# Strassen's weight sums made in place over two blocks, and one activation sum split into the double-buffered operand

## The chip, the cores and the metric

The kernel runs on one core of one Trainium2 chip. The metric is the device time of one execution in microseconds (us); the time of a kernel is the median of its runs. The core has a matrix engine (TensorE, PE in the profile), a vector engine (VectorE, DVE), a scalar engine (ScalarE, ACT), GpSimd (POOL) and a queue of DMA issues (SyncE, SP). Each engine takes its own instructions strictly in order; engines wait for each other by semaphores.

## The reference

Inputs and outputs are fp32 with 8 samples of 576 tokens and 512 channels. Three stages follow each other: a compressed attention, a mixer with two two-layer nets, and a mixture of four causal attention experts. The change lies in the second net of the mixer:

```python
u = x + h.transpose(0, 2, 1)
h2 = np.maximum(u @ w_ch1, 0.0) @ w_ch2      # w_ch1: 512 x 1536, w_ch2: 1536 x 512, given as 64-bit floats
return (u + h2).astype(np.float32)
```

## The kernel before

Every fp32 operand is split into a high part in the rounded type fp32r and the remainder (`split`: ScalarE rounds, VectorE subtracts); a product is then three matmuls, high x high, high x low and low x high (`mm3`). The 1536 hidden channels are 12 chunks of 128 (`fc`). Chunks 0 and 1 are done in the first stage, chunks 10 and 11 in the last one, chunks 2 to 9 in the stage of the change, which walks over 9 blocks of 512 tokens (`n`). The weights come as 64-bit floats, one load per chunk and matrix, into two staging buffers (`cst`), and are converted by a chain of steps on ScalarE and VectorE (`f64_split`, lines 120 to 129): line 120 on ScalarE and 124 on VectorE read a load that has landed, line 127 is the last to read it and so frees its staging buffer for the load after the next.

In blocks 0, 7 and 8 a chunk's hidden layer is a plain product (`mm1`); its eviction is `hh` on ScalarE (line 638) and `hl` on VectorE (line 639). In blocks 1 to 6 (`WIDE`) two chunks and two halves of the tokens are a 2 x 2 product of blocks, done in seven products instead of eight by the Strassen-Winograd scheme (`mm1w`). It needs, once for all blocks, four sums of weights for each of the four pairs of chunks `q` (`sums_w`: GpSimd joins the parts of both weights at line 655, makes four half-size sums at lines 659 to 663, and `split` makes `sh` and `sl` of them), and for each block four sums of activations (`split_q`: in place in `ub` on GpSimd, lines 679 to 685), each split once more: `split_t` makes `th` and `tl` of all four at the end of the block before, two of the `tl` on VectorE and two on GpSimd. `th` and `tl` have one buffer, so they wait until the last product of the block before has read them; the operand `uh`, `ul` of the plain quadrants has two. The products are added up on VectorE (lines 712 to 726) and evicted as `hh` and `hl` (lines 646 and 647). The second layer (`mm2`, four banks `o`) follows one step behind and is added to the partial result `pb` at the end of a block (line 742).

All weight sums are emitted in block 0, two steps per chunk. Their temporaries, two `x` and one `s` of four quarters, are a pool of their own (`stmp`), freed at the end of block 0; the temporaries `m1` to `m5` of the products (`uw`) then take its place. At the build a scheduler sets the order of each engine's instructions: it may place one far ahead of where it was emitted, as soon as its operands and its memory are free. So it has placed the first pairs' sums into the first stage, and the first steps of four loads for chunks 10 and 11 into block 0, although these chunks come hundreds of microseconds later.

## Time and profile before

| | |
|---|---|
| Time, median of 3 runs | 1232.45 us (1229.34 to 1232.87) |
| Profiled execution | 1230.86 us, of which the span from first to last instruction is 1229.2 |
| Busy share of the span | TensorE 97%, VectorE 66%, ScalarE 51%, GpSimd 37% |
| Block 0 on the trace | from 344 to 398 us, then block 1 |
| Granted TensorE clock, mean | 0.994 of full speed |

A matmul's end is modelled, so a row's duration is longer than the distance to the next one; what counts is where TensorE stands idle, and the distance of the starts. Engines other than TensorE may idle at no cost as long as nothing is late for it.

### The profile page before, as it was taken

Reading aid. Unit: us, or ns where it says so; the run is one execution under the profiler, and the core shown is the slowest. Engines: PE = TensorE matmul, PEld = TensorE weight load, DVE = VectorE, ACT = ScalarE, POOL = GpSimd, SP = SyncE. Lnnn points to the kernel's source line nnn. Section 1 sums busy time; section 2 is a strip of 40 time slices with the busy share of each in tenths; the row PEclk is TensorE's granted clock in tenths of the full one; section 3 lists DMA queues with packets and bytes.
Section 4 is the critical chain, followed back from the end, with each engine's and each line's share of the span. In section 5 each row is a group of like instructions: output and inputs, shape, how many; then the busy total and the mean of one; then the engine's idle time right before and its main releaser. Section 6 shows DMA issues by size and latency. Waiting matters only on the chain.

```text
span 1229.2 us, 24045 instructions
## 1 busy us (share of the span) xinstructions
PE 1186.2 (97%) x8730; PEld 1105.1 (90%) x8730; DVE 812.6 (66%) x1989; ACT 624.6 (51%) x1651; POOL 459.4 (37%) x646
## 2 busy tenths in 40 slices
PE   5789999999999999999999999999999999999998
PEld 4789999999987889888998888999999999999987
DVE  6877787886588676666555214676766766677774
ACT  3554656656344232222222113677676767676775
POOL 1432525446017122122105304454544546373421
PEclk9899999999999999999999999999999999999999
DMA  9875857753263231232134403332333233322423
GB/s 247 219 195 167 233 168 188 210 148 106 100 234 129 70 103 36 69 104 77 61 103 112 149 15 111 73 97 78 82 87 83 78 82 86 117 72 76 119 59 112
DMA packets 159765, 143.00 MB, mean 116 GB/s; under 512 B 73120, under 2 KB 128672, under 8 KB 159648
## 3 DMA queue, kind: packets, MB, share of 16 engines
q1 hardware_dynamic: 159648, 141.47, 39.8%
q8 instruction: 69, 1.13, 0.4%
q14 instruction: 48, 0.39, 0.1%
HBM read 90.05 MB, written 39.85 MB: 106 GB/s over the span
## 4 chain that ended last, share of the span: by engine, by line
PE 79%; DVE 5%; DMA 5%; POOL 3%; ACT 3%; issue 3%; SPq 1%; DVEq 0%; ACTq 0%; POOLq 0%
PE g L98 29%; PE o L98 13%; PE h L98 12%; PE b L98 8%; PE y L1134 4%; PE s L1025 2%; PE t L1089 2%; PE s L373 2%; DMA cst<-in_moe_w_ch_dram 2%; PE g L300 1%; PE s L1047 1%; DMA ub<-u_d 1%; DMA cst<-in_moe_w_tok_dram 1%; PE t L356 1%; PE g L468 1%
## 5 line engine op out<-in xcount | busy, mean ns | idle before, releaser
L98 PE MATMUL o<-hl,w2h 128*128 128x512 f32 x288 | 114.0, 396 | 2.5 <-DVE hl L639 2.3
L98 PE MATMUL o<-hh,w2l 128*128 128x512 f32 x288 | 113.1, 393 | 0.0
L1070 POOL TENSOR_TENSOR a<-a,cf 128x128 f32<-128x128 f32 (+3 forms) x128 | 88.1, 723 | 64.6 <-DVE cf L1062 56.5
L98 PE MATMUL o<-hh,w2h 128*128 128x512 f32 x288 | 108.3, 395 | 0.9 <-ACT hh L638 0.6
L646 ACT ACTIVATE hh<-m 128x256 fp32r<-128x256 f32 x96 | 38.7, 415 | 112.0 <-DVE m L717 74.3
L1014 DVE CUSTOM_DVE_ANT_0 ssb<-s,cmask 128x128 f32<-128x128 f32 (+2 forms) x144 | 68.4, 482 | 28.2 <-PE s L1025 14.1
L1027 ACT ACTIVATE a<-ssb,nb 128x128 f32<-128x128 f32 (+3 forms) x128 | 71.4, 558 | 19.1 <-DVE nb L1014 16.4
L389 POOL TENSOR_TENSOR at<-ssb,ssm 128x640 f32<-128x640 f32 x16 | 21.5, 1344 | 158.6 <-DVE ks L316 77.2
L923 POOL TENSOR_TENSOR xl<-p,xh 128x288 fp32r<-128x288 f32 x60 | 47.7, 811 | 84.1 <-ACT xh L922 84.0
L98 PE MATMUL g<-xh,qkh 128*128 128x288 f32 x256 | 76.1, 302 | 0.0
L98 PE MATMUL g<-xl,qkh 128*128 128x288 f32 x256 | 75.8, 297 | 0.0
L98 PE MATMUL g<-xh,qkl 128*128 128x288 f32 x256 | 75.1, 295 | 0.0
L647 DVE SCALAR_TENSOR_TENSOR hl<-m,hh 128x256 fp32r<-128x256 f32 x96 | 58.1, 615 | 17.3 <-ACT hh L646 15.6
L694 POOL TENSOR_TENSOR tl<-ub,th 128x512 fp32r<-128x512 f32 x12 | 18.5, 1562 | 133.2 <-ACT th L693 133.2
L98 PE MATMUL h<-ul,w1h 128*128 128x512 f32 (+2 forms) x200 | 66.8, 334 | 0.0
L98 PE MATMUL h<-uh,w1l 128*128 128x512 f32 (+2 forms) x200 | 66.8, 334 | 0.0
L98 PEld LDWEIGHTS o<-hl,w2h 128*128 128x128 f32 x288 | 54.6, 189 | 13.6 <-DVE hl L639 3.1
L98 PE MATMUL h<-uh,w1h 128*128 128x512 f32 (+2 forms) x200 | 66.6, 334 | 0.0
L98 PEld LDWEIGHTS o<-hh,w2h 128*128 128x128 f32 x288 | 54.0, 189 | 12.2 <-DVE pb L742 1.2
L98 PEld LDWEIGHTS o<-hh,w2l 128*128 128x128 f32 x288 | 54.5, 189 | 11.3
L105 DVE TENSOR_TENSOR Bl<-t,Bh 128x512 fp32r<-128x512 f32 (+1 forms) x80 | 50.4, 634 | 18.3 <-ACT Bh L102 17.4
L639 DVE SCALAR_TENSOR_TENSOR hl<-h,hh 128x512 fp32r<-128x512 f32 x24 | 16.5, 687 | 63.5 <-ACT hh L638 63.5
(325 smaller groups left out, 4382.7 us busy)
## 6 DMA issues: line engine op xcount, KB each, us to landing
cst<-in_moe_w_ch_dram SPq DMA_DIRECT2D x24, 512.0 KB, 4.9
u_d<-u SPq DMA_DIRECT2D x32, 288.0 KB, 2.2
p_d<-u SPq DMA_DIRECT2D x16, 576.0 KB, 3.5
ub<-u_d SPq DMA_DIRECT2D x9, 1024.0 KB, 5.3
pb<-p_d SPq DMA_DIRECT2D x36, 256.0 KB, 3.6
x_d<-pb SPq DMA_DIRECT2D x36, 256.0 KB, 2.2
u<-u_d SPq DMA_DIRECT2D x16, 576.0 KB, 4.2
p<-x_d SPq DMA_DIRECT2D x15, 576.0 KB, 4.0
```

The source lines that it names most:

```text
L98: PE.matmul(ps, lhsT=a, rhs=b, start=start and i == 0, stop=stop and i == len(seq) - 1)
L105: DVE.tensor_sub(lo, src, f(hi))
L373: PE.matmul(p[:, j, 2 * pr:2 * pr + 2, :], lhsT=qT[:, pr, 128 * j:128 * j + 128], rhs=km[:, 64 * pr:64 * pr + 64], start=True, stop=True)
L646: ACT.activation(hh, c, AF.Relu)
L647: DVE.scalar_tensor_tensor(hl, c, 0.0, f(hh), op0=OP.max, op1=OP.subtract)
L923: POOL.tensor_sub(xl[b][:, c, ss], x_, f(xh[b][:, c, ss]))
L1014: DVE.tensor_tensor_reduce(out=out, in0=p, in1=mask, scale=-scale, scalar=least, op0=OP.add, op1=OP.min, accum_out=acc)
L1025: PE.matmul(p[:, 0:W], lhsT=q_[n][:, 128 * c:128 * c + 128], rhs=kk[n][:, 0:W], start=(i == 0), stop=(i == 1))
L1027: ACT.activation(a[:, aoff[c]:aoff[c] + W], s_[:, 0:W], AF.Exp, scale=-1.0, bias=nb[:, 0:1], accum_out=sm[:, c:c + 1])
L1070: POOL.tensor_mul(x_, x_, cf[:, c:c + 1].to_broadcast([128, W]))
L1089: PE.transpose(p[:, 128 * kc:128 * kc + 128], a[:, o + 128 * kc:o + 128 * kc + 128], ident[:])
L1134: PE.matmul(p[:, lo:w], lhsT=v_[:, kc, 0, :], rhs=x, start=(i == 0), stop=(i == len(ops) - 1))
```

## The change

Three things change. The sums of weights use no `s` any more: each is made in place in the two `x`, which become four quarters that `split` reads in another order (`W` picks them by a table). The pairs are emitted in two blocks: pairs 0 and 1 in block 0 (one step per chunk from the third on), pairs 2 and 3 in block 1 (`SOON = 2`), and the pool of temporaries stays open with the operands. Weight conversion steps are emitted two per chunk instead of one. And of the four sums of activations, the one that is the second product's operand (quadrant 2,2 of `ub` after its sum) is split in `split_q` into the fourth quadrant of `uh`, `ul`, which was unused; `th` and `tl` shrink from four quarters to three, of which VectorE makes two `tl` and GpSimd one.

```diff
--- before.py
+++ after.py
@@ -655,16 +655,16 @@
                 POOL.tensor_add(t[:], f(w1h[fc][:]), f(w1l[fc][:]))
             yield
             a11, a12, a21, a22 = x[0][:, 0:2, :], x[0][:, 2:4, :], x[1][:, 0:2, :], x[1][:, 2:4, :]
-            s_ = stmp.tile([128, 4, 2, 128], F32, name="s")
-            POOL.tensor_add(s_[:, 0], a21, a22)
-            POOL.tensor_sub(s_[:, 1], s_[:, 0], a11)
+            POOL.tensor_add(a22, a21, a22)
+            POOL.tensor_sub(a21, a11, a21)
             yield
-            POOL.tensor_sub(s_[:, 2], a11, a21)
-            POOL.tensor_sub(s_[:, 3], a12, s_[:, 1])
+            POOL.tensor_sub(a11, a22, a11)
+            POOL.tensor_sub(a12, a12, a11)
             sh[q] = sw.tile([128, 4, 2, 128], F32R, name=f"sh{q}")
             sl[q] = sw.tile([128, 4, 2, 128], F32R, name=f"sl{q}")
             for i in range(2):
-                split(sh[q][:, 2 * i:2 * i + 2], sl[q][:, 2 * i:2 * i + 2], s_[:, 2 * i:2 * i + 2])
+                split(sh[q][:, 2 * i:2 * i + 2], sl[q][:, 2 * i:2 * i + 2],
+                      x[i][:].rearrange("p (s c) f -> p s c f", s=2))
             yield
 
         def quad(x, j, k):
@@ -683,21 +683,22 @@
             POOL.tensor_sub(q22, q22, q11)
             yield
             POOL.tensor_sub(q21, q21, q22)
+            split(quad(uh[n], 0, 1), quad(ul[n], 0, 1), q22)
             yield
 
         def split_t(n):
-            th[n] = sw.tile([128, 4, 2, 256], F32R, name="th")
-            tl[n] = sw.tile([128, 4, 2, 256], F32R, name="tl")
-            q11, q12, q21, q22 = [quad(ub[n], j, k) for j in range(2) for k in range(2)]
-            for i, q_ in ((1, q22), (2, q12), (0, q11), (3, q21)):
+            th[n] = sw.tile([128, 3, 2, 256], F32R, name="th")
+            tl[n] = sw.tile([128, 3, 2, 256], F32R, name="tl")
+            q11, q12, q21 = [quad(ub[n], j, k) for j, k in ((0, 0), (0, 1), (1, 0))]
+            for i, q_ in ((1, q12), (0, q11), (2, q21)):
                 ACT.activation(th[n][:, i], q_, AF.Copy)
-                (DVE if i in (1, 2) else POOL).tensor_sub(tl[n][:, i], q_, f(th[n][:, i]))
+                (POOL if i == 2 else DVE).tensor_sub(tl[n][:, i], q_, f(th[n][:, i]))
 
         def mm1w(n, q):
             f0, f1 = N1 + 2 * q, N1 + 2 * q + 1
             A = lambda fc, j: [x[fc][:, 2 * j:2 * j + 2, :] for x in (w1h, w1l)]
             U = lambda j, k: [quad(x[n], j, k) for x in (uh, ul)]
-            W = lambda i: [x[q][:, i] for x in (sh, sl)]
+            W = lambda i: [x[q][:, (3, 0, 2, 1)[i]] for x in (sh, sl)]
             X = lambda i: [x[n][:, i] for x in (th, tl)]
 
             def prod(pool, a, b):
@@ -708,9 +709,9 @@
             m1, u2_, u3, u4, c = [uw.tile([128, 256], F32, name=x, bufs=2)[:] for x in ("m1", "m2", "m3", "m4", "m5")]
             p = prod(pp, A(f0, 0), U(0, 0))
             ACT.activation(m1, p, AF.Copy)
-            p = prod(pp, W(1), X(1))
+            p = prod(pp, W(1), U(0, 1))
             DVE.tensor_add(u2_, m1, p)
-            p = prod(ppw, W(2), X(2))
+            p = prod(ppw, W(2), X(1))
             DVE.tensor_add(u3, u2_, p)
             p = prod(ppw, W(0), X(0))
             DVE.tensor_add(u4, u2_, p)
@@ -718,7 +719,7 @@
             p = prod(pp, A(f0, 1), U(1, 0))
             hidden(n, f1, 1, c)
             DVE.tensor_add(m1, m1, p)
-            p = prod(pp, A(f1, 1), X(3))
+            p = prod(pp, A(f1, 1), X(2))
             hidden(n, f0, 0, m1)
             DVE.tensor_add(u3, u3, p)
             p = prod(ppw, W(3), U(1, 1))
@@ -788,16 +789,17 @@
             split_u(0, kd)
         load_u(1)
         b1_ctx.close()
-        sw_ctx, tmp_ctx = ExitStack(), ExitStack()
+        sw_ctx = ExitStack()
         sw = sw_ctx.enter_context(tc.tile_pool(name="sw", bufs=1, side="right", reuse_waits="tile"))
         ppw = sw_ctx.enter_context(tc.tile_pool(name="ppw", bufs=1, space=PSUM, side="right", reuse_waits="tile"))
-        stmp = tmp_ctx.enter_context(tc.tile_pool(name="stmp", bufs=1, side="right", reuse_waits="tile"))
+        stmp = sw_ctx.enter_context(tc.tile_pool(name="stmp", bufs=1, side="right", reuse_waits="tile"))
         NQP = (KM - N1) // 2
         WIDE = range(1, NBLK - 2)
+        SOON = 2
         work = [(n, q) for n in range(NBLK) for q in range(NQP)]
         LAG = 1
         NW = len(work)
-        pending, sprep = [], (x for q in range(NQP) for x in sums_w(q))
+        pending, sprep = [], iter(())
         uw = None
         for i in range(NW + LAG):
             items = [()] if i == NW else [work[i]] if work[i][0] in WIDE else [(*work[i], 0), (*work[i], 1)]
@@ -809,6 +811,8 @@
                         banks(n)
                         prep = iter(()) if n + 1 == NBLK else split_q(n + 1) if n + 1 in WIDE else \
                             (split_u(n + 1, kd) for kd in range(KD))
+                        if n < 2:
+                            sprep = (x for k in range(*((0, SOON), (SOON, NQP))[n]) for x in sums_w(k))
                     if len(it) == 2:
                         mm1w(n, q)
                     else:
@@ -820,8 +824,9 @@
                             load_p(n, fc - KM + KD)
                         if n == 0:
                             next(wcl, None)
-                            for _ in range(2):
-                                next(sprep, None)
+                            next(wcl, None)
+                        if n == 1 or n == 0 and fc > N1 + 1:
+                            next(sprep, None)
                         if n > WIDE[-1]:
                             for _ in range(4):
                                 if next(wcl, 0) == 0 and c2 is None:
@@ -836,8 +841,10 @@
                             for g in (wcl, sprep):
                                 for _ in g:
                                     pass
-                            tmp_ctx.close()
                             uw = sw_ctx.enter_context(tc.tile_pool(name="uw", bufs=1, side="right", reuse_waits="tile"))
+                        if n == 1:
+                            for _ in sprep:
+                                pass
                         if n + 1 in WIDE:
                             split_t(n + 1)
                         if n + 2 < NBLK:
```

How the scheduler's order moves is shown for three places. The first is ScalarE in the second half of block 0. In the rows `hh<-h` are the evictions of hidden chunks 7, 8 and 9, `sh` the copies of weight sums, and `cm<-cst` is line 120 on the hoisted loads, each of which has its own semaphore (DMAHW4, 5, 6 in the order of issue). Before:

```order
L638 ACTIVATE hh<-h 128x512 [waits PE_49,Activation_49]
L120 ACTIVATE cm<-cst 128x512 [waits DMAHW4_49]
L102 ACTIVATE sh_5273<-s 128x512 [waits Pool_49]
L120 ACTIVATE cm<-cst 128x512 [waits DMAHW5_49,DVE_49]
L102 ACTIVATE sh_5273<-s 128x512 [waits Pool_49]
L638 ACTIVATE hh<-h 128x512 [waits PE_49,Activation_49]
L120 ACTIVATE cm<-cst 128x512 [waits DMAHW6_49,DVE_49]
L102 ACTIVATE sh_5320<-s 128x512 [waits Pool_49] x2
L638 ACTIVATE hh<-h 128x512 [waits PE_49,Activation_49]
```

The same place on ScalarE now:

```order
L120 ACTIVATE cm<-cst 128x512 [waits DMAHW4_49]
L638 ACTIVATE hh<-h 128x512 [waits PE_49,Activation_49]
L102 ACTIVATE sh_5352<-x_5281 128x512 [waits DMAHW3_49,DMAHW0_49,Pool_49]
L120 ACTIVATE cm<-cst 128x512 [waits DMAHW5_49,DVE_49]
L102 ACTIVATE sh_5352<-x_5280 128x512 [waits Pool_49]
L120 ACTIVATE cm<-cst 128x512 [waits DMAHW6_49,DVE_49]
L638 ACTIVATE hh<-h 128x512 [waits PE_49,Activation_49]
L102 ACTIVATE sh_5570<-x_5465 128x512 [waits Pool_49]
L102 ACTIVATE sh_5570<-x_5464 128x512 [waits Pool_49]
L638 ACTIVATE hh<-h 128x512 [waits PE_49,Activation_49]
```

The evictions of chunks 7 and 8 each stand behind one more of the loads' steps, and the copies of the fourth pair (5320 before) have gone further down.

The second is GpSimd, from the last of the in-place sums for block 1 on (`ub<-ub`); `x` and `s` are the temporaries, their numbers those of the pairs. Before, with the first pair and half of the second already done in the first stage:

```order
L685 TENSOR_TENSOR ub<-ub 128x2x256 [waits DVE_49,Pool_49]
L659 TENSOR_TENSOR s<-x_5148 128x256 [waits DVE_49]
L662 TENSOR_TENSOR s<-x_5147,x_5148 128x256
L694 TENSOR_TENSOR tl<-ub,th 128x512 [waits PE_49,Activation_49]
L694 TENSOR_TENSOR tl<-ub,th 128x512 [waits Activation_49]
L660 TENSOR_TENSOR s<-s,x_5147 128x256 [waits Pool_49]
L655 TENSOR_TENSOR x_5232<-w1h_4834,w1l_4835 128x512 [waits Pool_49]
L663 TENSOR_TENSOR s<-x_5147,s 128x256 [waits Pool_49]
L655 TENSOR_TENSOR x_5231<-w1h_3318,w1l_3319 128x512 [waits Pool_49]
```

The same place on GpSimd now:

```order
L685 TENSOR_TENSOR ub<-ub 128x2x256 [waits DVE_49,Pool_49]
L655 TENSOR_TENSOR x_5170<-w1h_854,w1l_855 128x512 [waits DMAHW5_49,DMAHW6_49,DMAHW3_49,DMAHW7_49,DMAHW2_49,DMAHW0_49]
L655 TENSOR_TENSOR x_5171<-w1h_882,w1l_883 128x512
L695 TENSOR_TENSOR tl<-ub,th 128x512 [waits PE_49,Activation_49]
L658 TENSOR_TENSOR x_5171<-x_5171 128x256 [waits Pool_49]
L659 TENSOR_TENSOR x_5171<-x_5170,x_5171 128x256 [waits Pool_49]
L661 TENSOR_TENSOR x_5170<-x_5171,x_5170 128x256 [waits Pool_49]
L662 TENSOR_TENSOR x_5170<-x_5170 128x256 [waits Pool_49]
L655 TENSOR_TENSOR x_5281<-w1h_2084,w1l_2085 128x512 [waits DVE_49]
L658 TENSOR_TENSOR x_5281<-x_5281 128x256 [waits Pool_49]
L655 TENSOR_TENSOR x_5280<-w1h_2029,w1l_2030 128x512 [waits DVE_49]
```

All four pairs stand behind the sums for block 1 now, each full-size sum waits for VectorE to have read the same buffer for the pair before, and one `tl` is gone.

The third is VectorE at the start of block 1, from the first sum of the products on; `m` are the sums, `pb` the additions at the end of block 0, `ul<-ub` a split of the sums of activations for block 2. Before:

```order
L712 TENSOR_TENSOR m_5424<-m_5423,h 128x256 [waits PE_49,Activation_49]
L742 TENSOR_TENSOR pb<-o_5086,pb 128x512 [waits PE_49]
L714 TENSOR_TENSOR m_5425<-m_5424,h 128x256 [waits DVE_49]
L716 TENSOR_TENSOR m_5426<-m_5424,h 128x256
L742 TENSOR_TENSOR pb<-o_5087,pb 128x512 [waits PE_49]
L742 TENSOR_TENSOR pb<-o_5088,pb 128x512 [waits PE_49]
L717 TENSOR_TENSOR m_5427<-m_5425,h 128x256 [waits DVE_49]
L742 TENSOR_TENSOR pb<-o_5089,pb 128x512 [waits PE_49]
L720 TENSOR_TENSOR m_5423<-m_5423,h 128x256 [waits PE_49]
L723 TENSOR_TENSOR m_5425<-m_5425,h 128x256 [waits DVE_49,PE_49]
L647 SCALAR_TENSOR_TENSOR hl<-m_5427,hh 128x256 [waits Activation_49]
L726 TENSOR_TENSOR m_5426<-m_5426,h 128x256 [waits PE_49]
```

The start of block 1 on VectorE now:

```order
L105 TENSOR_TENSOR sl_5692<-x_5579,sh_5691 128x512 [waits Activation_49]
L713 TENSOR_TENSOR m_5391<-m_5390,h 128x256 [waits PE_49,Activation_49]
L105 TENSOR_TENSOR sl_5692<-x_5578,sh_5691 128x512 [waits Activation_49]
L715 TENSOR_TENSOR m_5392<-m_5391,h 128x256 [waits DVE_49]
L717 TENSOR_TENSOR m_5393<-m_5391,h 128x256 [waits PE_49]
L743 TENSOR_TENSOR pb<-o_5086,pb 128x512 [waits PE_49]
L718 TENSOR_TENSOR m_5394<-m_5392,h 128x256 [waits DVE_49]
L743 TENSOR_TENSOR pb<-o_5087,pb 128x512 [waits PE_49]
L721 TENSOR_TENSOR m_5390<-m_5390,h 128x256 [waits PE_49]
L743 TENSOR_TENSOR pb<-o_5088,pb 128x512 [waits PE_49]
L105 TENSOR_TENSOR ul<-ub,uh 128x2x256 [waits Activation_49]
L647 SCALAR_TENSOR_TENSOR hl<-m_5394,hh 128x256 [waits Activation_49]
```

The two `sl` of the fourth pair and the new split stand among the first pair's sums and ahead of its first `hl`.

## Rows read from the trace of the kernel before

**Rows 1.** Three stretches: busy us (and instructions) of each engine, granted clock, DMA.
```profile
380.00:390.00 10.00, 8.11 (x32) 6.04 (x31) 9.30 (x10) 2.94 (x5) 8.69 (x8) 0.90 0.62 210
390.00:400.00 10.00, 9.61 (x45) 7.68 (x43) 7.49 (x9) 5.42 (x10) 6.97 (x8) 0.93 0.16 53
...
450.00:460.00 10.00, 10.00 (x61) 8.64 (x60) 7.32 (x17) 1.58 (x4) 1.23 (x1) 1.00 0.63 210
```

**Rows 2.** Waits of TensorE, 310 to 660 us: us in total, times, longest.
```profile
PE o L98 <- DVE hl L639: 2.3, 2, 1.9
PE h L98 <- DVE m L717: 0.9, 1, 0.9
...
PE o L98 <- ACT hh L638: 0.6, 1, 0.6
PE o L98 <- DVE pb L742: 0.3, 1, 0.3
```

**Rows 3.** Timeline of TensorE: start, us, instruction [idle before <-releaser].
```profile
388.08 0.80 PE L98 MATMUL o<-hl,w2h 128*128 128x512 f32 x1 [1.90 <-DVE hl L639]
...
391.23 0.45 PE L98 MATMUL o<-hh,w2h 128*128 128x512 f32 x1
...
391.97 0.40 PE L98 MATMUL h<-uh,w1h 128*128 128x512 f32 x1
...
394.49 0.39 PE L98 MATMUL h<-uh,w1l 128*128 128x512 f32 x1
```

**Rows 4.** Timeline of VectorE, block 0.
```profile
359.64 1.51 DVE L121 TENSOR_SCALAR cm<-cm 128x512 f32<-128x512 f32 x1
...
363.11 0.41 DVE L121 TENSOR_SCALAR cm<-cm 128x512 f32<-128x512 f32 x1
...
377.58 1.52 DVE L124 TENSOR_SCALAR cy<-cst 128x512 int32<-128x512 uint32 x1
...
379.61 1.18 DVE L127 SCALAR_TENSOR_TENSOR cy<-cst,cm 128x512 int32<-128x512 int32 x1
...
387.01 0.41 DVE L124 TENSOR_SCALAR cy<-cst 128x512 int32<-128x512 uint32 x1
...
387.35 0.68 DVE L639 SCALAR_TENSOR_TENSOR hl<-h,hh 128x512 fp32r<-128x512 f32 x1
```

**Rows 5.** Timeline of the DMA queue: issues of two weight loads.
```profile
380.87 0.34 SPq L152 DMA_DIRECT2D cst<-in_moe_w_ch_dram  x1
...
393.09 0.34 SPq L152 DMA_DIRECT2D cst<-in_moe_w_ch_dram  x1
```

**Rows 6.** Timeline of ScalarE, block 0.
```profile
372.99 0.57 ACT L638 ACTIVATE hh<-h 128x512 fp32r<-128x512 f32 x1
...
386.84 0.67 ACT L120 ACTIVATE cm<-cst 128x512 f32<-128x512 f32 x1 [1.45 <-DMA cst<-in_moe_w_ch_dram]
...
393.05 0.58 ACT L638 ACTIVATE hh<-h 128x512 fp32r<-128x512 f32 x1
...
396.70 0.67 ACT L120 ACTIVATE cm<-cst 128x512 f32<-128x512 f32 x1 [3.07 <-DMA cst<-in_moe_w_ch_dram]
```

**Rows 7.** Timeline of GpSimd, end of the first stage and block 0.
```profile
274.49 2.52 POOL L655 TENSOR_TENSOR x<-w1h,w1l 128x512 f32<-128x512 f32 x2 [6.58 <-DVE w2l L129]
...
286.75 1.28 POOL L655 TENSOR_TENSOR x<-w1h,w1l 128x512 f32<-128x512 f32 x1
...
359.25 1.62 POOL L683 TENSOR_TENSOR ub<-ub 128x512 f32<-128x512 f32 x1
...
360.95 1.35 POOL L685 TENSOR_TENSOR ub<-ub 128x512 f32<-128x512 f32 x1
...
373.11 2.05 POOL L659 TENSOR_TENSOR s<-x 128x256 f32<-128x256 f32 x1 [10.80 <-DVE sl L105]
...
377.26 2.99 POOL L694 TENSOR_TENSOR tl<-ub,th 128x512 fp32r<-128x512 f32 x2
...
397.34 0.75 POOL L663 TENSOR_TENSOR s<-x,s 128x256 f32<-128x256 f32 x1
```

## What is predicted

> **What bounds the kernel now.** I read the page's first table, then a table by stretches, then the waits of TensorE, then each engine in order of time where TensorE waited. In the first TensorE fills nearly the whole span, so only time in which it waits or runs slow can be won, or lost by a new wait. The stretches show where that is in the stage that the change touches: from 380 to 400 us TensorE is busy 8.11 and 9.61 of 10 us at a granted clock of 0.90 and 0.93, while VectorE is busy 9.30 and 7.49; at 450, between two wide blocks, it is busy all the time [rows 1]. So the loss sits in block 0 and at the start of block 1 (from 400 us), not in the wide blocks that follow.
>
> The list of TensorE's waits from 310 to 660 us names it: 2.3 us for `hl` of line 639 in two waits, 0.6 for `hh` of line 638, 0.9 for a sum of line 717, and 0.3 at a later block border [rows 2]. The 1.9 us wait costs twice: the seven steps from the matmul of 388.08 to that of 391.23 are 0.45 us each, the eleven from 391.97 to 394.49 0.23 us; the first run at about half the pace, which is the lower of TensorE's two levels (1.2 GHz), right behind the wait, and that adds 7 x 0.22 = 1.6 us [rows 3]. Together 0.6 + 2.3 + 1.6 + 0.9 = 5.4 us: more than that block 0 and its border cannot give back.
>
> Why is `hl` late? VectorE takes its instructions in order. `hl` of 387.35 stands behind a conversion step of line 124 that waits for a weight load [rows 4]; the load was issued at 380.87 [rows 5], and ScalarE, which waits for the same load, goes on at 386.84, 6.0 us later; the next such pair is 393.09 and 396.70, 3.6 us [rows 5, 6]. Four such loads are for the last two hidden chunks, which nobody needs in this stage. The second thing in VectorE's way is GpSimd: line 121 takes 0.41 us alone at 363.11, but 1.51 us at 359.64, ending 0.28 us after the GpSimd instruction that ran from 359.25 to 360.87 [rows 4, 7]. Conversely GpSimd's half-size sum takes 0.75 us at 397.34 and 2.05 us at 373.11, where VectorE works without a gap [rows 7].
>
> **The change part by part.**
>
> *Sums in place.* The number of GpSimd sums is the same: 8 full-size (two take 2.52 us, so 1.26 each) and 16 half-size ones (0.75) [rows 7]. But they move in time. Before, four full-size and four half-size ones run between 274.49 and 288 us, in the first stage (the first and the last of these rows stand in [rows 7]). In the changed order all stand behind the four in-place sums of activations, the last of which begins at 360.95 [rows 7]. So 4 x 1.26 + 4 x 0.75 = 8 us of GpSimd work comes into block 0. GpSimd was idle from 362.3 to 373.11 [rows 7], which hides the first two full-size sums (2.5 us); they now meet VectorE's conversions there, where line 121 ran in 0.41 us. By row 359.64 a VectorE step then loses up to 1.1 us, by row 373.11 none, GpSimd waits instead: bounds 0 and 2.5 us on the conversion chain, and I take 1.
>
> The Trainium skill (SBUF — State Buffer, section "Who interferes with whom") says that whichever of the two engines issues first holds the shared port for its whole instruction, for a VectorE step with two SBUF inputs too. By that every one of the moved sums can push the chain; the chain would slip by the upper bound here, and the trace shows both outcomes (1.51 us at 359.64, and GpSimd's own 2.05 us at 373.11).
>
> *Place a, hidden chunk 5.* Two `sh` and one `th` copy go from ahead of `hh` of 372.99 [rows 6], so the 0.6 us wait for it goes. But the seven matmuls of block 1 that TensorE had put between `hh` and `hl` (they need the first `sh`) now come later, and `hl` is hardly earlier (two `sl` fewer, one split more). TensorE asks for it about 0.9 us after 372.3, it comes at about 374.4: a wait of 1.2 us instead of 0.6. Change +0.6 (bounds -0.6 and +1.5).
>
> *Place b, chunk 6.* `hh` now stands behind the first `sh`, that is behind GpSimd. +0.4 (0 to 2).
>
> *Place c, chunk 7.* Today 1.9 + 1.6 us. In the new order `hl` stands behind three steps of the load of 380.87 instead of one, 0.41 + 0.68 us more, and `hh` behind ScalarE's step on that load. But the load starts earlier: its buffer is released by the line 127 of 379.61, which took 1.18 us, and the line 124 of 377.58 ahead of it 1.52, both behind the two `tl` sums of 377.26 on GpSimd [rows 4, 7]; only one of those is left, and it comes sooner. Without it the two take 0.41 and 0.68, and the load goes 1.6 us earlier, at 379.2. With 4.8 us of flight (the middle of 3.6 and 6.0) and 2.4 us of steps, `hl` is ready at 386.4; TensorE asks at 385.1, counted from 372.3 with 49 matmuls of 0.23 us and the waits of a and b. A wait of 1.3 (0 to 2.6) and some slow clock: 2.0 instead of 3.5. Change -1.5 (-3.5 to 0).
>
> *Place d, chunk 8.* This is the step on which my sign rests. Before, `hh` of 393.05 stands ahead of ScalarE's step on the last load, which goes at 396.70 [rows 6]. In the changed order it stands behind it, and `hl` behind VectorE's step on it. That load's buffer is released only by the line 127 that comes right after `hl` of place c. So from `hl` of c to `hh` of d it takes 0.6 + 3.6 to 6.0 + 0.7 + 0.6 = 5.5 to 7.9 us, more with GpSimd in the way, where TensorE has 23 matmuls of 0.23 us, 5.3 us. A wait of 0.2 to 3.8 us; I take 2.0, with 0.8 of slow clock, instead of 0.4 + 0.1 now. Change +2.3.
>
> *Start of block 1.* The sums of the fourth pair now begin after `sl` of the third, right behind `hl` of d, and mix with the in-place sums for block 2. VectorE and ScalarE in turn have a copy of the fourth pair ahead of the first sums of the products, and a split of `ub` (it waits for the third in-place sum of block 2) ahead of the first `hl`. Counting from `hl` of d with 1.26 and 0.75 us, the fourth pair's second half is ready after 7.5 us and that split after 11.4; TensorE asks for the buffers that hang on them after 9.1, 10.5 and 12.6 us and gets them after about 9.3, 11.8 and 13.0: 1.9 us in three waits, and 5.5 with the mutual slowing of the rows of 359.64 and 373.11. Today 0.9 [rows 2]. I take 3.7; change +2.8 (+1.0 to +4.6).
>
> *Split into the double-buffered operand.* In each of blocks 2 to 6 GpSimd has one `tl` less (1.5 us, the half of 377.26 [rows 7]) and VectorE one split more, which now is made one block earlier instead of at the border. No wait for `tl` is among TensorE's in the wide blocks [rows 2], so nothing is won there. But the extra split falls where the border's sums and additions are, VectorE busy 7.32 of 10 us [rows 1], and the wait listed there is 0.3 us. +0.1 a border on five borders, +0.5 (from -1.5, all of it gone, to +3.5, the whole 0.7 us of the split each time).
>
> Sum: 0.6 + 0.4 - 1.5 + 2.3 + 2.8 + 0.5 = +5.1 us. The profiled execution took 1230.86 us (span 1229.2 and 1.66 around it), so 1236.0 by its measure; the median of the runs, 1232.45, lies 1.6 higher: 1237.5.
>
> **The rivals.** A measurement of this kernel can tell about 0.3%, 3.7 us.
>
> *Traded even.* a to c go as above, but block 1 starts without the mutual slowing (1.9 instead of 3.7), d is served by a 3.6 us flight (0.5 instead of 2.8) and the borders stay: 0.6 + 0.4 - 1.5 + 0.1 + 1.0 + 0.5 = +1.1, so 1233.5. For it speaks that only the short bounds are shown as such by rows; against it that VectorE is busy over 9 of 10 us around 385.
>
> *Faster.* GpSimd starts its sums at 362.3 instead of 373.1, all pairs are ready early, the queue ahead of `hl` shrinks and the long wait with its slow clock never happens. Then a and c give back 0.6 + 3.5, the start of block 1 0.9, and the five borders 0.2 each: -6, so 1226.5. It holds from the point where no wait in block 0 passes 1 us. For it: the idle 10.8 us are real. Against it: every later pair waits for the `sl` of the pair before, so an early start doesn't carry through, and the loads order the chunks anyway.
>
> *Slower by the port.* Each moved sum pushes the conversion chain, as at 359.64, and never the other way round: b +1.4, c -0.3, d +3.8, block 1 +4.6, borders +1.0, with a +11, so 1243.5. It decides from the point where the chain slips by more than 2 us before c. The rule of the Trainium skill named above points this way.
>
> **How the numbers follow.** Forecast (a wait that moves one load nearer and a late fourth pair, +3.7 to +8): 0.40; traded even: 0.35; faster: 0.15; slower by the port: 0.10. Faster by over 0.3%: 0.15; within: 0.37 (the even case and a little of the forecast's lower end); slower: 0.48. The forecast's own range is 1235 to 1241. The range for 8 in 10 leaves out half of the faster case and half of the port case: 1228 to 1244.
>
> **What would show it.** In the changed profile GpSimd's line 655 should begin near 362, not 274; the wait for `hh` at 373 should be gone and one for `hl` stand there; a wait of 1 to 3 us for `hh` or `hl` of line 638 and 639 should end right after ScalarE's step on the last load (place d), and waits for sums of the products should total 2 to 5 us between 400 and 420. If `hh` of d is served before TensorE asks, or the stretch from 400 to 420 is busy throughout, I am wrong and the even or the faster case holds. If the wide borders show more than 0.7 us each, the term of the split was too small.

## The result

The changed kernel took 1239.81 us, median of 4 runs (1237.29 to 1241.30), against 1232.06 of the kernel before; the ratio is 1.0060, 95% interval 1.0045 to 1.0074, so 5.5 to 9.1 us slower, 7.4 in the middle. The forecast was 1237.5 us, +5.1.

The profiled execution took 1237.29 us (span 1235.6), 6.4 more than the one of before. To see where, I counted the matmuls in both traces and compared the start of the same number:

| from matmul to matmul | what lies there | before | after | difference |
|---|---|---|---|---|
| up to 900 | first 100 us | to 103.4 | to 101.2 | -2.2 |
| 900 to 3,150 | first stage | 103.4 to 355.8 | 101.2 to 353.6 | 0.0 |
| 3,150 to 3,318 | block 0 | 355.8 to 397.9 | 353.6 to 398.9 | +3.1 |
| 3,318 to 3,450 | start of block 1 | 397.9 to 419.2 | 398.9 to 426.3 | +6.2 |
| 3,600 to 5,250 | wide blocks and what follows | 443.0 to 732.7 | 450.1 to 738.9 | -0.9 |
| 5,250 to 6,000 | start of the last stage | 732.7 to 841.0 | 738.9 to 847.9 | +0.7 |

The first line is no part of the change: the two kernels' instructions have the same order there, and in the profiles of the twelve other kernels below this stretch differs from before by -1.0 to +3.4 us. Matmuls 3,450 to 3,600 differ by 0.0 us, and what lies behind 6,000 by -0.5. What is left, +9.3 from block 0 to the start of block 1, is what is to be explained. (A few short matmuls of block 1 stand in block 0 in one order and not in the other, so the line between the two is good to about 0.7 us.)

The stretches of the changed kernel, 20 us each [rows 1 show the same view]:

```profile
360.00:380.00 20.00, 14.84 (x57) 11.29 (x56) 18.39 (x26) 7.37 (x15) 9.24 (x8) 0.91 0.44 143
380.00:400.00 20.00, 20.00 (x90) 16.61 (x90) 16.27 (x21) 8.57 (x15) 15.30 (x15) 0.92 0.30 98
400.00:420.00 20.00, 15.84 (x82) 13.65 (x82) 14.78 (x28) 4.80 (x12) 10.15 (x8) 0.83 0.32 106
```

TensorE (first number after the comma) stands idle at two places, 360 to 380 and 400 to 420, and the granted clock (the third number from the end) is 0.91, 0.92 and 0.83. Before, the one bad stretch was 380 to 400. The list of its waits from 310 to 660 us, the answer to [rows 2]:

```profile
PE o L98 <- DVE hl L639: 4.0, 2, 3.1
PE h L98 <- DVE m L715: 1.9, 1, 1.9
PE h L98 <- DVE m L724: 1.1, 1, 1.1
PE o L98 <- ACT hh L638: 1.1, 1, 1.1
PE h L98 <- ACT m L711: 0.9, 1, 0.9
...
PE h L98 <- DVE m L718: 0.3, 1, 0.3
```

The first, `hl` of line 639, are chunks 4 and 5 of block 0; the `m` are the first products of block 1. Chunks 6, 7 and 8 have no wait at all. What made `hl` of chunk 4 and 5 late is seen on GpSimd and VectorE, the answers to [rows 7] and [rows 4]. GpSimd:

```profile
360.64 3.18 POOL L655 TENSOR_TENSOR x<-w1h,w1l 128x512 f32<-128x512 f32 x2
372.18 1.59 POOL L695 TENSOR_TENSOR tl<-ub,th 128x512 fp32r<-128x512 f32 x1 [8.36 <-ACT th L694]
373.73 1.17 POOL L658 TENSOR_TENSOR x<-x 128x256 f32<-128x256 f32 x1
```

VectorE in the same time:

```profile
360.90 1.78 DVE L125 SCALAR_TENSOR_TENSOR cm<-cm,cy 128x512 int32<-128x512 int32 x1
362.60 1.51 DVE L121 TENSOR_SCALAR cm<-cm 128x512 f32<-128x512 f32 x1
...
364.39 0.68 DVE L127 SCALAR_TENSOR_TENSOR cy<-cst,cm 128x512 int32<-128x512 int32 x1
...
365.96 0.68 DVE L639 SCALAR_TENSOR_TENSOR hl<-h,hh 128x512 fp32r<-128x512 f32 x1
...
370.05 0.43 DVE L121 TENSOR_SCALAR cm<-cm 128x512 f32<-128x512 f32 x1 [1.61 <-ACT cm L120]
...
372.54 1.78 DVE L127 SCALAR_TENSOR_TENSOR cy<-cst,cm 128x512 int32<-128x512 int32 x1
374.24 1.21 DVE L695 TENSOR_TENSOR tl<-ub,th 128x512 fp32r<-128x512 f32 x1
375.37 0.94 DVE L124 TENSOR_SCALAR cy<-cst 128x512 int32<-128x512 uint32 x1
376.24 0.68 DVE L639 SCALAR_TENSOR_TENSOR hl<-h,hh 128x512 fp32r<-128x512 f32 x1
```

The two full-size sums of 360.64 take 1.59 us each instead of 1.26 [rows 7], and VectorE's steps beside them 1.78 and 1.51 instead of 0.68 and 0.41: 2.2 us lost. The line 127 of 364.39 releases the staging buffer for chunk 9's load, which is issued at 365.15 and whose step on ScalarE (line 120) runs at 369.36; VectorE waits 1.61 us for it. From 372.54 on GpSimd's `tl` and half-size sums cost VectorE 2.2 us once more (1.78 + 1.21 + 0.94 against 0.68 + 0.68 + 0.41). So `hl` of chunk 5 comes 3.1 us after TensorE asks. TensorE itself, the answer to [rows 3]:

```profile
376.97 0.80 PE L98 MATMUL o<-hl,w2h 128*128 128x512 f32 x1 [3.14 <-DVE hl L639]
377.56 0.63 PE L98 MATMUL o<-hh,w2l 128*128 128x512 f32 x1
...
383.11 0.40 PE L98 MATMUL h<-uh,w1h 128*128 128x512 f32 x1
383.35 0.40 PE L98 MATMUL h<-ul,w1h 128*128 128x512 f32 x1
```

Behind the wait 13 steps (377.56 to 383.11) are 0.43 us apart, the lower level of 1.2 GHz, then 0.23: 13 x 0.2 = 2.6 us more. With the waits of 0.9 (chunk 4), 1.1 (`hh` of chunk 5) and 3.1 that makes 7.7 us in block 0, against 0.6 + 2.3 + 1.6 = 4.5 before [rows 2, 3]: +3.2, where the table has +3.1. The 1.1 us for `hh` have the same source: on ScalarE it stands behind line 120 on chunk 9's load (369.36) and three copies `th`.

At the start of block 1 the fourth pair is what is late. GpSimd first, then ScalarE, which waits for it, then TensorE:

```profile
401.58 1.07 POOL L659 TENSOR_TENSOR x<-x,x 128x256 f32<-128x256 f32 x1
...
403.74 1.74 POOL L679 TENSOR_TENSOR ub<-ub 128x512 f32<-128x512 f32 x1
405.44 0.74 POOL L662 TENSOR_TENSOR x<-x 128x256 f32<-128x256 f32 x1
```

```profile
402.68 0.63 ACT L102 ACTIVATE sh<-x 128x512 fp32r<-128x512 f32 x1 [2.62 <-POOL x L659]
403.22 0.37 ACT L711 ACTIVATE m<-h 128x256 f32<-128x256 f32 x1
406.21 0.63 ACT L102 ACTIVATE sh<-x 128x512 fp32r<-128x512 f32 x1 [2.63 <-POOL x L662]
```

```profile
403.64 0.39 PE L98 MATMUL h<-uh,w1h 128*128 128x256 f32 x1 [0.86 <-ACT m L711]
408.34 0.39 PE L98 MATMUL h<-uh,sh 128*128 128x256 f32 x1 [1.86 <-DVE m L715]
413.33 0.58 PE L98 MATMUL h<-uh,sh 128*128 128x256 f32 x1 [1.15 <-DVE m L724]
...
413.92 0.41 PE L98 MATMUL h<-uh,sl 128*128 128x256 f32 x1
...
415.84 0.41 PE L98 MATMUL h<-uh,w1l 128*128 128x256 f32 x1
```

With the 0.29 for line 718 these are 4.2 us of waits, and the matmuls of 256 columns from 413.92 to 415.84 are 0.21 us apart (nine steps) where they were 0.12 at 404, again the lower level. That lasts from 410.53 to 417.12, for 24 of them: 24 x 0.09 = 2.2 us of slow clock. 4.2 + 2.2, less the 0.9 of before, are 5.5 of the +6.2; the other 0.7 are as much as the line between the two blocks is good to.

### The profile page after: what moved, and what is told of

Same layout as the page of the kernel before. It is cut to its first block, busy times and chain, and to the rows that moved or that the text cites. A ratio compares the mean times of both kernels' runs of the same rounds, so it can differ in the third digit from the quotient of the medians.

```text
span 1235.6 us, 24036 instructions
## 1 busy us (share of the span) xinstructions
PE 1188.6 (96%) x8730; PEld 1108.8 (90%) x8730; DVE 815.5 (66%) x1995; ACT 625.4 (51%) x1651; POOL 449.6 (36%) x640
## 4 chain that ended last, share of the span: by engine, by line
PE 74%; DVE 11%; DMA 6%; ACT 3%; POOL 3%; issue 2%; SPq 1%; DVEq 0%; ACTq 0%; POOLq 0%
PE g L98 29%; PE o L98 10%; PE h L98 10%; PE b L98 8%; PE y L1141 4%; PE t L1096 2%; PE s L1032 2%; DMA cst<-in_moe_w_ch_dram 2%; PE s L373 2%; DVE ul L105 2%; DMA ub<-u_d 2%; PE g L300 1%; PE s L1054 1%; DVE pb L743 1%; PE t L356 1%
## 5 line engine op out<-in xcount | busy, mean ns | idle before, releaser
L695 POOL TENSOR_TENSOR tl<-ub,th 128x512 fp32r<-128x512 f32 x6 | 9.9, 1649 | 151.2 <-ACT th L694 151.2
L647 DVE SCALAR_TENSOR_TENSOR hl<-m,hh 128x256 fp32r<-128x256 f32 x96 | 53.7, 573 | 13.1 <-ACT hh L646 11.5
```

The source lines that it names most:

```text
L647: DVE.scalar_tensor_tensor(hl, c, 0.0, f(hh), op0=OP.max, op1=OP.subtract)
```

## The experiments

Each kernel was timed in five rounds beside the kernel before. Two parts of the diff needed no run: with all four pairs emitted in block 0 (`SOON = NQP`, two steps a chunk), or with one conversion step per chunk as before, the scheduler puts out the same sequence of instructions on every engine as for the changed kernel. "Over two blocks" and the second `next(wcl)` do nothing.

**The split alone, in two sizes.** The sums of weights stay as before.

```diff
-            th[n] = sw.tile([128, 4, 2, 256], F32R, name="th")
+            th[n] = sw.tile([128, 3, 2, 256], F32R, name="th")
...
+            split(quad(uh[n], 0, 1), quad(ul[n], 0, 1), q22)
```

> The kernel before with the split into the double-buffered operand alone (th, tl of three quarters); the sums of weights keep their temporary s and are all emitted in block 0. Because th and tl are smaller, the temporaries of the sums lie elsewhere in memory, and every sum of weights stands behind the four in-place sums of activations, as in the changed kernel. Theory A (place: the loss in block 0 is GpSimd's full-size sums starting right behind the in-place sums, while VectorE converts): line 655 begins near 360 us, VectorE's steps beside it take 1.5 to 1.8 us instead of 0.4 to 0.7, TensorE waits for hl of chunk 4 by about 0.9 and for hl of chunk 5 by 2 to 3.5 us, block 0 loses 7 to 9 us; the start of block 1 loses 1 to 4; time +3 to +6 us over before. Theory B (chain: the loss is that each pair, made in place, waits for VectorE to have read the pair before): without in-place sums block 0 loses 4 to 5 us as before, time -1 to +1. Theory C (the split itself costs at each border of a wide block): +0.7 us a border, visible as waits there, time +3 or more with block 0 unchanged.

Ratio 1.0066 (1.0050 to 1.0083), +8.1 us: the whole loss, without any sum made in place, and more than the +3 to +6 of theory A, since the start of block 1 loses 5.7 us more than before and not 1 to 4. GpSimd and VectorE on its trace:

```profile
362.64 3.17 POOL L655 TENSOR_TENSOR x<-w1h,w1l 128x512 f32<-128x512 f32 x2
```

```profile
362.88 1.77 DVE L125 SCALAR_TENSOR_TENSOR cm<-cm,cy 128x512 int32<-128x512 int32 x1
364.58 1.51 DVE L121 TENSOR_SCALAR cm<-cm 128x512 f32<-128x512 f32 x1
```

The same with `th` and `tl` left at four quarters, one of them unused:

> As the run with the split alone, but th and tl keep four quarters, the fourth unused, so that the temporaries lie where they lay before and the first pair and a half are again made in the first stage. Theory A (place): block 0 loses 4 to 5 us as before, the wide borders lose nothing, time -1.5 to +1 us against before; against the run with the split alone 3 to 6 us less. Theory B (chain): the same as the run with the split alone, both within 1 us of before. Theory C (split): +3 us or more, in both alike, with waits at the borders of the wide blocks.

Ratio 0.9999 (0.9987 to 1.0011): nothing. On its trace the sums are back in the first stage, and the steps short:

```profile
273.58 2.53 POOL L655 TENSOR_TENSOR x<-w1h,w1l 128x512 f32<-128x512 f32 x2 [6.62 <-DVE w2l L129]
```

```profile
361.46 0.68 DVE L125 SCALAR_TENSOR_TENSOR cm<-cm,cy 128x512 int32<-128x512 int32 x1
362.06 0.41 DVE L121 TENSOR_SCALAR cm<-cm 128x512 f32<-128x512 f32 x1
```

The two programs as written differ in 4 KB per partition and nothing else. The smaller `th` and `tl` move the temporaries of the sums to other memory, and there the scheduler puts the first sum behind line 685 (in the changed kernel it waits for six DMA queues besides). Theory A holds here, B and C fall: in the padded kernel the wide blocks win 1.7 us against before (matmuls 3,600 to 5,250) and the start of the last stage loses 0.7, and in the time nothing of it is seen: the split itself is worth less than the interval, about 1.5 us either way.

**In place alone**, all pairs in block 0, `th` and `tl` of four quarters:

```diff
-            s_ = stmp.tile([128, 4, 2, 128], F32, name="s")
-            POOL.tensor_add(s_[:, 0], a21, a22)
-            POOL.tensor_sub(s_[:, 1], s_[:, 0], a11)
+            POOL.tensor_add(a22, a21, a22)
+            POOL.tensor_sub(a21, a11, a21)
```

> The kernel before with the in-place sums of weights alone: no s, th and tl of four quarters, no split into the double-buffered operand; the first pair is still made in the first stage, the second pair's two full-size sums come behind the in-place sums of activations. Theory A (place): two full-size sums of GpSimd meet VectorE's conversions behind 360 us, as in the changed kernel, but the first pair is ready; block 0 loses 5 to 8 us, the start of block 1 1 to 3; time +1 to +4. Theory B (chain): the later pairs wait for VectorE as in the changed kernel, block 0 loses 7 to 9 us and the start of block 1 5 to 7, time +6 to +8, as the whole change.

Ratio 1.0028 (1.0017 to 1.0040), +3.5: the time and the losses of theory A (block 0 loses 1.6 us more than before, the start of block 1 another 1.8), with one pair early instead of one and a half. But the collision is not where the theory put it. The next full-size sums don't start behind 360 us: GpSimd stands idle for 10.35 us until VectorE's `sl` has read `x`, and makes them at 372.68, ahead of its own two `tl`; beside this work VectorE's two `tl` take 3.43 us instead of 1.29. TensorE waits 3.0 us for that `tl` of line 694 and 1.6 for an `hh`, and for `hl` of line 639 only 0.4. The time is below theory B's +6 to +8, but that a pair waits for VectorE is B's link: in this kernel both are at work.

**The changed kernel with its pools in another order:**

```diff
+        uw = sw_ctx.enter_context(tc.tile_pool(name="uw", bufs=1, side="right", reuse_waits="tile"))
         stmp = sw_ctx.enter_context(tc.tile_pool(name="stmp", bufs=1, side="right", reuse_waits="tile"))
...
-                            uw = sw_ctx.enter_context(tc.tile_pool(name="uw", bufs=1, side="right", reuse_waits="tile"))
```

> The changed kernel with the pool of the products' temporaries opened ahead of that of the sums' temporaries, nothing else: these then lie elsewhere, and the first pair is made in the first stage. Theory A (place): the wait for hl of chunk 4 goes, that for chunk 5 falls below 2 us, block 0 loses 4 to 6 us instead of 8; the start of block 1 stays at 5 to 7; time +3 to +5 over before, 3 to 4 less than the changed kernel. Theory B (chain): pairs 2 to 4 still wait for VectorE; time as the changed kernel, +6 to +8.

Ratio 1.0023 (1.0011 to 1.0034), +2.8, just under the +3 to +5 of theory A: 4.6 us of the 7.4 come back from moving one line. The wait for chunk 4 is gone. Waits of 1.5 and 3.1 stay, but now at chunks 6 and 7, block 0 loses 2.1 us more than before, and the start of block 1 only 1.0, not the 5 to 7 that theory A expected: with one pair early the later ones are nearly in time.

**ScalarE copies instead of GpSimd's full-size sums**, in the changed kernel:

```diff
-                POOL.tensor_add(t[:], f(w1h[fc][:]), f(w1l[fc][:]))
+                ACT.activation(t[:], f(w1h[fc][:]), AF.Copy)
```

> The changed kernel, but the eight full-size sums of line 655 are copies of the high part on ScalarE, so the low parts of the weights are left out of the sums of weights. Place, pairs and in-place sums stay as in the changed kernel; GpSimd loses 8 x 1.3 us, ScalarE gains 8 x 0.6. Theory A1 (port: the full-size sums slow VectorE's steps beside them): the steps from 359 to 365 us take 0.4 to 0.7 us, the wait for hl of chunk 4 goes, that of chunk 5 falls to 1.5 us or less, block 0 loses 3 to 5 us instead of 8, the start of block 1 1 to 4; time 0 to +3 us over before. Theory B (queue: it is the order on VectorE and ScalarE, with sl and sh of late pairs ahead of hh and hl): the waits stay within 1 us, time +6 to +8.

This kernel leaves the low parts of the weights out of their sums. Ratio 0.9991 (0.9981 to 1.0002), -1.1 us: without those eight sums on GpSimd the change costs nothing. Its DMA issues keep the order of the changed kernel, which from 284 us on is another than before, so that order is not the loss. VectorE beside the empty place, and TensorE's waits:

```profile
362.40 0.68 DVE L125 SCALAR_TENSOR_TENSOR cm<-cm,cy 128x512 int32<-128x512 int32 x1
```

```profile
PE o L98 <- DVE hl L639: 2.6, 1, 2.6
PE o L98 <- ACT hh L638: 1.0, 1, 1.0
...
PE h L98 <- DVE m L721: 0.6, 1, 0.6
PE h L98 <- DVE m L724: 0.3, 1, 0.3
```

Chunk 4's wait is gone, block 1's are down from 4.2 to 1.2. Chunk 5's is still 2.6, not 1.5 or less as expected: there GpSimd's `tl` and half-size sums are enough, as in the changed kernel from 372.18. B falls. How much of the 8.5 us between the two is the mutual slowing and how much GpSimd's own time for the late pairs, this run doesn't part, since it takes away both.

**The loads of chunks 10 and 11 later**, in the kernel before:

```diff
-            s_ = spool.tile([128, wd, 2], I32, name="cst", bufs=nb)[:, 0:DM, :]
+            s_ = (cpool or spool).tile([128, wd, 2], I32, name="cst", bufs=nb)[:, 0:DM, :]
...
+                            stg3 = stg3_ctx.enter_context(tc.tile_pool(name="stg3", bufs=2, side="right"))
...
-                yield from ch_weights(w3, stg, fc, DM, 2)
+                yield from ch_weights(w3, stg, fc, DM, 2, cpool=stg3)
```

> The kernel before, with a staging buffer of their own for the weights of chunks 10 and 11, in memory that is free only after block 6, so that their four loads and conversion steps leave block 0 and come in blocks 7 and 8; nothing else moves. Theory L (the wait of 1.9 us for hl at 388 and the slow clock behind it come from these loads in VectorE's queue): the waits of chunks 7 and 8 go, block 0 loses 0.5 to 1.5 us instead of 4.5, blocks 7 and 8 lose nothing; time -2.5 to -4.5 us. Rival (GpSimd's sums by the port are what makes hl late, the loads only stand nearby): a wait of 1 us or more for hl of chunk 6 or 7 stays, time -1 to +0.5.

Ratio 0.9969 (0.9954 to 0.9983), -3.8 us. The waits from 310 to 660 us, against [rows 2]:

```profile
PE h L98 <- DVE tl L694: 0.9, 1, 0.9
PE b L98 <- DVE hl L176: 0.7, 1, 0.7
PE o L98 <- ACT hh L638: 0.6, 1, 0.6
...
```

No `hl` of line 639 any more, nor an `m`; what is left out is 0.3 us or less each. The reading of the kernel before (`hl` behind a conversion that nobody needs yet) is shown. The same in the changed kernel:

> The changed kernel with the same separate staging buffer: the four loads of chunks 10 and 11 leave block 0. Theory L: chunk 7 and 8 had no wait in the changed profile, so nothing is won there; the wait of 3.1 us for hl of chunk 5 stands behind chunk 9's load and one of these four, and falls to 1.5 to 2.5; with VectorE freer the pairs 3 and 4 are ready earlier and the start of block 1 loses 2 to 4 us instead of 7; time +1 to +4 over before. Rival (place and port decide all of it): block 0 loses 7 to 8 and the start of block 1 5 to 7 as in the changed kernel, time +6 to +8.

Ratio 1.0040 (1.0027 to 1.0054), +4.9: 2.5 us won of 7.4, short of what L expected, since chunk 5's wait is 3.1 as ever (it hangs on chunk 9's load and on GpSimd) and the start of block 1 still loses 4.4 us more than before, where the changed kernel loses 6.2. With the pools in the other order too:

> The changed kernel with the pool of the products' temporaries opened first (the first pair is made in the first stage) and the loads of chunks 10 and 11 after block 6. If place and loads are separate costs that add: +2.8 of the first alone, less the 3 to 4.6 that the loads gave so far, so -2 to +0.5 us against before. If they hide each other (VectorE freed of the loads only waits for GpSimd instead): +2 to +3, as with the pool moved alone.

Ratio 0.9994 (0.9983 to 1.0005), -0.7 us: place (+2.8) and loads (-3.8 in the kernel before, -2.5 in the changed one) would give -1.0 or +0.3, so they add as far as the interval tells. The waits do not: a new one of 3.2 us for `tl` of line 695 stands in chunk 5. And in the padded split:

> The split alone with th and tl padded to four quarters (sums of weights early, as before), and the loads of chunks 10 and 11 after block 6: the version that the runs so far point to. If the loads are what block 0 waits for, -3 to -5 us against before, and within 1 us of the kernel before with the loads later; if the split has a worth of its own in the wide blocks, 0.5 to 1 us better than that one. Rival: block 0's waits come back elsewhere, -1 to +1.

Ratio 0.9968 (0.9954 to 0.9982), 1227.66 us against 1227.52 of the kernel before with the loads later: the two best versions, equal, both faster than before and than the changed kernel. The expected 0.5 to 1 us of the split is not there.

**More pairs early.** In place with `x` double-buffered, in the memory that `x` and `s` had; the scheduler puts two whole pairs into the first stage.

```diff
-            x = [stmp.tile([128, KD, 128], F32, name=f"x{i}") for i in range(2)]
+            x = [stmp.tile([128, KD, 128], F32, name=f"x{i}", bufs=2) for i in range(2)]
```

> The kernel before with the in-place sums of weights alone, and x double-buffered, in the memory that x and s had: the first two pairs (four full-size, eight half-size sums) are made in the first stage, before it was one and a half, and a pair no longer waits for VectorE to have read the one before. Theory A (what counts is how many of GpSimd's sums are left to block 0): no more than before, time -2 to +0.5 us, 3 to 5 less than in place with single x. Theory B (in place itself costs, by dependences within a pair): time +2 to +4, as with single x.

Ratio 1.0005 (0.9996 to 1.0013), +0.6: 2.9 us less than with a single `x`, so in place itself costs nothing, but also not better than before, though GpSimd has less to do in block 0: TensorE now waits 4.3 us for `tl` of line 694 in chunk 5. With the loads later, and then with the split too:

> In-place sums with x double-buffered, two pairs made in the first stage, and the loads of chunks 10 and 11 after block 6; no split into the double-buffered operand. The best that theory A offers: -4.5 to -6.5 us against before, block 0 and the start of block 1 together under 1.5 us of waits. If in place itself costs: -2 to 0.

> As the run before it, with the split into the double-buffered operand too (th and tl padded to four quarters, so that the place stays). The split alone, padded, made no difference to before, so within 1 us of the run without it; 0.5 to 1 us less if the 0.9 us that the changed profile wins at one wide border is real.

1.0009 (0.9999 to 1.0018) and 1.0009 (0.9997 to 1.0022). A miss by 6 us: the 3.8 that the loads gave in the kernel before are not here. The wait for `tl` is the same as without them. ScalarE, VectorE and TensorE of the first of the two:

```profile
370.60 2.18 ACT L102 ACTIVATE sh<-x 128x512 fp32r<-128x512 f32 x4
372.68 2.17 ACT L693 ACTIVATE th<-ub 128x512 fp32r<-128x512 f32 x4
```

```profile
375.11 2.37 DVE L105 TENSOR_TENSOR sl<-x,sh 128x512 fp32r<-128x512 f32 x2
377.41 3.42 DVE L694 TENSOR_TENSOR tl<-ub,th 128x512 fp32r<-128x512 f32 x2
```

```profile
373.86 0.90 PE L98 MATMUL h<-th,sh 128*128 128x256 f32 x2 [1.32 <-ACT th L693]
380.88 0.58 PE L98 MATMUL h<-tl,sh 128*128 128x256 f32 x1 [3.42 <-DVE tl L694]
```

With two pairs ready there are four `sh` ahead of `th` on ScalarE and four `sl` ahead of `tl` on VectorE, and TensorE's own order has a product of block 1, with `th` and `tl`, in the middle of chunk 5. So TensorE waits 4.7 us there for a product that block 1 needs only some 25 us later. Sums that come early are no gain by themselves.

## Why the prediction was right, and where it was wrong

The sign, the place (block 0 and the start of block 1) and nearly the size were right: +5.1 against 7.4. That is partly luck, since single terms were off in both directions, and the step on which I rested the sign failed. ScalarE and TensorE at place d of the changed kernel:

```profile
393.43 0.66 ACT L120 ACTIVATE cm<-cst 128x512 f32<-128x512 f32 x1 [3.58 <-DMA cst<-in_moe_w_ch_dram]
394.00 0.58 ACT L638 ACTIVATE hh<-h 128x512 fp32r<-128x512 f32 x1
```

```profile
395.55 0.62 PE L98 MATMUL o<-hh,w2h 128*128 128x512 f32 x2
```

In the list, "and the 2.2" means that the 2.2 us by which the changed kernel is ahead since the first 100 us are added to the difference of two times.

- *Sums in place* (I took 1 us on the conversion chain, between 0 and 2.5): mis-sized, and no line of my sum shows where the 1 us went in. It measured 2.2 at 360.90 and 2.2 again at 372.54; `hl` of chunk 7 begins 3.4 us later than before (388.50 against 387.35, and the 2.2). That is past the 2 us from which the rival *slower by the port* was to decide. Its terms for b and d (+1.4, +3.8) did not come, and the time lies between the forecast and that case: the first link of the loss is that rival's. The reason that I gave for it, that all sums stand behind line 685, was right, and the comparison of the padded with the unpadded split shows that it carries the loss. What moved them I had not seen as a matter of 4 KB of `th` and `tl`.
- *Place a* (+0.6, up to +1.5): too small by far. Chunk 4 gained a wait that I didn't have (0.9), chunk 5 has 1.1 for `hh` and 3.1 for `hl`, with 2.6 of slow clock: 7.7 in all against 0.6 before. I had the wait for `hh` gone, and it grew. The chain's slip had turned into a later load for chunk 9.
- *Place b* (+0.4): no wait.
- *Place c* (-1.5, at most -3.5): all of it went, since TensorE asks 6.4 us later (390.34 against 386.18, and the 2.2), `hl` comes only 3.4 later, and is ready.
- *Place d* (+2.3), the step on which I rested my sign: it failed. The last load's step runs on ScalarE at 393.43, `hh` behind it at 394.00, as foreseen, but TensorE asks only at 395.55 and does not wait. A wait that comes earlier in the same chain had used it up. By my own sign (`hh` of d served before TensorE asks) the even or the faster case had to hold; neither did, because the loss had moved ahead of d. I added the four places as if each began from the time of before; they share one chain, and the sum over block 0 (+3.1 against my +1.8) is what can be compared.
- *Start of block 1* (+2.8, at most +4.6): the waits are those foreseen, for the fourth pair's copies among the first sums and for the split of `ub` ahead of line 724, 4.2 us against 3.7. I left out that the clock falls behind them, 2.2 us more; the table has +6.2.
- *Borders* (+0.5): -0.9, no loss; the 0.3 us wait for `pb` [rows 2] is gone. The +0.7 at the start of the last stage was in none of my terms. All nine kernels with the split win 0.9 to 1.8 us in the wide blocks, and seven of them lose 0.6 or 0.7 at the start of the last stage; what causes the latter is open.

The rule of the Trainium skill (SBUF — State Buffer, "Who interferes with whom") pointed the right way at the first collision: VectorE's steps lost 1.1 us each beside the full-size sums. The trace agrees, and it shows that with both queues full both engines pay: GpSimd's sums took 1.59 instead of 1.26 us, and the VectorE step of 362.60 ended 0.29 us after the second of them (364.11 against 363.82), as if the two took turns. Which of them held the port when, the rows do not show.

## What to carry to other kernels

Where a scheduler places work by free memory, the size of a tile can decide when other work runs: look at which instructions change their place when a pool shrinks, before costing the edit itself. Waits along one in-order chain don't add: cost them in order, each from the time that the one before leaves, and add the slow clock that the rows show behind the longer ones. And look for work in the critical queues that nobody needs yet: moving four early loads out of block 0 won 3.8 us in the kernel before, more than any part of this change did, 2.5 in the changed one, and nothing where another wait in the same queues took over.

## What the runs showed of the hardware that I had not expected

- The first 100 us vary by several us from one profile to the next (-2.2 to +3.4 against before, over thirteen kernels with the same order of instructions there), so one profile's span can't tell 3 us; the same matmul's start in two traces can.
- With `x` double-buffered and the loads later, two `tl` on VectorE took 3.42 us at 377.41, beside GpSimd's sum and its own two `tl` (1.29 in the kernel before, at 373.28, with a half-size sum beside them), while those two on GpSimd took 3.40 (2.99 before, at 377.26). So VectorE slowed by 2.7 times, and GpSimd by 1.1.
